# Keys and queries of six head pairs, transposed into one PSUM bank, copied by ScalarE and placed by two transfers

## The chip, the cores and the metric

The kernel runs on one core of a Trainium2 chip. Times are device microseconds of one execution, and the metric is their median over several runs: 278.72 us before the change, of three runs of 278.40, 278.72 and 280.70. One more execution was profiled. A core has TensorE (PE; its weight loads are shown as PEld), VectorE (DVE), ScalarE (ACT), GpSimd (POOL) and SyncE (SP). Matmuls write to PSUM, a memory of banks of 2 KB for each of 128 partitions; the other engines copy from there to SBUF. POOL, SP and ACT also issue DMA transfers.

## What is computed

Attention in which each query sees only some chunks of keys, and behind it a feed-forward layer. Shapes: 4 batches, 8 heads, 768 tokens, head dimension 64; the layer has 512 inputs and 2048 hidden units.

```python
k_chunks = k.reshape(B, H, nc, chunk, D)          # 24 chunks of 32 keys
k_min, k_max = np.min(k_chunks, axis=3), np.max(k_chunks, axis=3)
ub = np.sum(np.maximum(q[:, :, :, None, :] * k_min[:, :, None], 
                       q[:, :, :, None, :] * k_max[:, :, None]), axis=-1)
ub = np.where(causal, ub, -1e9)
top_chunks = np.argsort(ub, axis=-1)[..., -6:]
scores = scale * q @ k.T                          # where chunk selected and causal
out = softmax(scores) @ v
h = np.maximum(x @ w_in, 0.0)                     # x: out of all heads, 3072 x 512
return h * h @ w_out
```

## The kernel before

The work is cut into 32 pairs of heads: a batch, a half of its tokens (384), and two heads, in the order of `slots` (L208). Four pairs make a half batch (a group). The kernel's order is written out by hand: `tile_...` records for each engine its instructions in the order in which the Python calls stand, and each engine runs its own list in that order, waiting where an operand isn't there. Pairs are counted from 0; "slot s" is the turn of the main loop (L681) for pair s.

In slot s stand, by calls in this order: scores and exponentials of pair s (`step_E`, L395: matmuls into `ps`, ScalarE's `Exp` to `e`, for some parts a causal mask on POOL), the bounds of pair s+1 (`step_U`, L345), the output product of pair s-1 (`step_F`, L420: `po`, then a reciprocal and a product on VectorE to `x`), more scores, the selection of pair s+1 (`step_V`, L368: transposes `qt`, copied by VectorE beside the queries at L393 and L394), and the transposes of pair s+2 (`step_P`, L336). Between them `f1` puts pieces of the feed-forward layer from a queue: four matmuls of an up-projection (`ph`, L522; then `Relu` on ScalarE, square on VectorE at L528), or four of a down-projection (`py`, L538).

What becomes of a pair's keys and queries, for pairs 4 to 11: `step_T` (L235) transposes them on TensorE, 16 small matmuls, into two tiles, `tk` and `tq`, of one PSUM bank each; tokens stand there in the order (j p), four interleaved runs, and not (p j) as they are wanted. From PSUM four things are made. `relus_T` (L262): ScalarE writes relu(-q) and relu(q), in token order, to `qr` (L271). `extrema` (L212): VectorE reduces each chunk of 32 keys to its minimum and maximum (L216, L217) and multiplies them with a mask into `kbd` (L218). `place` (L273, the copies are at L276): VectorE copies the keys, and ScalarE the queries, head by head in token order to `kqs`, from which the score matmuls read; head 0 lies in partitions 64 to 127, head 1 in 0 to 63, while in PSUM head 0 is in 0 to 63. The bounds are matmuls of `qr` with `kbd` (L354); VectorE takes the eight largest of them (L361) and compares (L362, `nsel`).

Where the parts stand: `step_P` does `step_T` and, from pair 6 on, `step_T2` (L255), which is relus, extrema, both placings. For pair 9 the transposes are in slot 7 and the rest is written out in slot 8 (L713 to L728), between transposes of `x` (`x_T`, L460) and their copies (L472). Pairs 0 to 5 have code of their own. Pairs from 12 on are transposed by DMA from SP (`tr`, L302) into `kqT`, placed by two transfers for four pairs (`place_dma`, L286), and their relus are VectorE's, from SBUF (`relus`, L293, L299 and L300); the transfers of pairs 12 to 15 are issued in slots 9 to 11.

PSUM has eight banks: pool `psS` three (tag "ps"), `psF` two, `psY` one ("py"), `psA` two ("att"; also for `ub`, `qt`, `po`). `step_P` puts keys and queries of pairs 6 to 8 into psY and psS, those of pairs 9 to 11 into psS and psA.

Of the kernel before, what the change touches and what calls it, by code (L numbers as in the profile page):

```python
# [9 lines left out]
BF16 = mybir.dt.bfloat16  # L10
AX = mybir.AxisListType
ALU = mybir.AluOpType
# [5 lines left out]
HB = HT * 128  # L18
# [10 lines left out]
ORDER = ((0, 0), (1, 0), (0, 1), (1, 1), (2, 0), (2, 1), (3, 0), (3, 1))  # L29
# [3 lines left out]
TP = 4  # L33
# [6 lines left out]
def kernel(  # L40
# [9 lines left out]
    nc = tc.nc  # L50
    B, H, S, D = q.shape
    NC = S // CH
    NT = S // 128
    NP = H // 2
# [7 lines left out]
    work = ctx.enter_context(tc.tile_pool(name="work", bufs=2))  # L62
# [32 lines left out]
    def packed(n, g):  # L95
        return nat_of(n, g)[0:PP, :].rearrange("p (h x) -> p h x", h=H)
# [73 lines left out]
    for g in range(4):  # L170
        for j in range(HT):
            c = 13 + g + 4 * j
# [35 lines left out]
    slots = [(b, half, p) for b, half in ORDER for p in range(NP)]  # L208
    NS = len(slots)
    st = {}  # L210

    def extrema(kt, s):  # L212
        b, half, p = slots[s]
        km = work.tile([128, 2, 12], BF16, tag="km", name="km")
        kv = kt.rearrange("r (j c e) -> r c j e", j=TP, c=12)
        nc.vector.tensor_reduce(km[:, 0, :], kv, axis=AX.XY, op=ALU.min)  # L216
        nc.vector.tensor_reduce(km[:, 1, :], kv, axis=AX.XY, op=ALU.max)  # L217
        nc.vector.tensor_mul(  # L218
            kbds[b % 2][:, p, :, :, 12 * half:12 * half + 12], hmask,
            km.unsqueeze(2).to_broadcast([128, 2, 2, 12]))  # L220

    def in_order(x):

        return x.rearrange("r (j p) -> r p j", j=TP)

    def by_token(x):
        return x.rearrange("r (p j) -> r p j", j=TP)
# [7 lines left out]
    def step_T(s, kp, qp):  # L235

        b, half, p = slots[s]
        t = st.setdefault(s, {})
        for n, (pool, tag) in zip("kq", (kp, qp)):
            x = t[n] = pool.tile([128, HB], BF16, tag=tag, name="t" + n)  # L240
            if n == "q" and s < NP:
                for j in range(HT):
                    nc.tensor.matmul(
                        x[:, 128 * j:128 * (j + 1)],
                        lhsT=qn0[:, j, p, 1:3, :].rearrange("p h d -> p (h d)"),
                        rhs=ident, is_transpose=True, start=True, stop=True)
                continue
            for hh in range(2):
                for j in range(TP):
                    nc.tensor.matmul(  # L250
                        x[D * hh:D * hh + D, PP * j:PP * j + PP],
                        lhsT=packed(n, s // NP)[:, 2 * p + hh, D * j:D * j + D],
                        rhs=ident[0:PP, 0:PP], is_transpose=True, start=True, stop=True)

    def step_T2(s):  # L255
        relus_T(s)
        extrema(st[s]["k"], s)
        if s >= NP:
            place(s, "k", nc.vector.tensor_copy)
            place(s, "q", nc.scalar.copy)  # L260

    def relus_T(s):  # L262
        b, half, p = slots[s]
        t = st[s]
        qr = t["qr"] = work.tile([128, 2, HB], BF16, tag="qr", bufs=3, name="qr")
        c = 128 * (1 - half)
        for w in range(2):
            o, i = qr[:, w, c:], t["q"][:, c:]
            if s >= NP:
                o, i = by_token(o), in_order(t["q"])[:, c // TP:, :]  # L270
            nc.scalar.activation(o, i, ACT.Relu, scale=(-1.0, 1.0)[w])  # L271

    def place(s, n, copy, h0=0, h1=2):  # L273
        b, half, p = slots[s]
        for h in range(h0, h1):
            copy(by_token(kqs[b % 2][QROW[h]:QROW[h] + D, h, p, 2 * half + "kq".index(n), :]),  # L276
                 in_order(st[s][n][D * h:D * h + D]))

    tT = {}
# [11 lines left out]
                in_=half_T(g)[D * h:D * h + D])  # L291

    def relus(s):  # L293
        g, p = s // NP, s % NP
        qT = tT[g][:, p, 1, :]
        c = 128 * (1 - ORDER[g][1])
        t = st.setdefault(s, {})
        qr = t["qr"] = work.tile([128, 2, HB], BF16, tag="qr", bufs=3, name="qr")
        nc.vector.tensor_scalar(qr[:, 0, c:], qT[:, c:], -1.0, 0.0, op0=ALU.mult, op1=ALU.max)  # L299
        nc.vector.tensor_scalar_max(qr[:, 1, c:], qT[:, c:], 0.0)  # L300
# [31 lines left out]
    F, Y, A = (psF, "ph"), (psY, "py"), (psA, "att")  # L332

    S_ = (psS, "ps")

    def step_P(s):  # L336
        if s // NP >= ON_PE:
            relus(s)
            return
        step_T(s, *((S_, Y) if s == NP + 1 else (F, Y) if s < NP + 2 else  # L340
                    (Y, S_) if s < 2 * NP + 1 else (S_, A)))
        if s >= NP + 2 and s != 2 * NP + 1:
            step_T2(s)

    def step_U(s):  # L345
        b, half, p = slots[s]
# [113 lines left out]
    def x_T(hb, g, pt, us=(0, 1)):  # L460

        if (hb, g) not in pts:
            pts[hb, g] = pt[0].tile([128, 2, HB], BF16, tag=pt[1], name="pt")
        for u in us:
            for j in range(HT):
                nc.tensor.matmul(
                    pts[hb, g][:, u, 128 * j:128 * (j + 1)],
                    lhsT=xs[hb][:, j, 128 * (2 * g + u):128 * (2 * g + u + 1)],
                    rhs=ident, is_transpose=True, start=True, stop=True)
# [80 lines left out]
    def fill(n, act):  # L550
        for _ in range(n):
            if queue:
                queue.pop(0)(act)
# [127 lines left out]
    for s, (b, half, p) in enumerate(slots):  # L681
        if s < NP:
            continue
        hb = s // NP
        nb = len(BANKS[half])
        hf = nb // 2
        quota = [((4, 4, 4, 4) if hb == 1 else (8, 6, 7, 7))[p]]
        for fn, *a in first.get(s, ()):
            fn(*a)
        if ON_PE - 1 <= hb < 2 * B - 1 and p == (2 if hb < ON_PE else 1):  # L690
            parts.extend(step_K(hb + 1))

        def f1():
            if quota[0] and queue:
                quota[0] -= 1
                fill(1, True)

        if s == NP:
            for n in range(hf):
                step_E(s, 0, n)  # L700
            step_F(s - 1, 0)
            step_F(s - 1, 1)
            relus_T(s + 1)
            x_T(0, 1, F, (0,))
            x_copy(0, 1, 0, 1, nc.vector.tensor_copy)
            busy(8, *A)
            x_T(0, 1, F, (1,))
            x_copy(0, 1, 1, 2, nc.vector.tensor_copy)
            push(0)
            extrema(st[s + 1]["k"], s + 1)  # L710
            place(s + 1, "k", nc.vector.tensor_copy)
            place(s + 1, "q", nc.scalar.copy)
        if s == 2 * NP:  # L713
            for n in range(hf):
                step_E(s, 0, n)
            relus_T(s + 1)
            place(s + 1, "q", nc.scalar.copy)
            x_T(1, 0, A)
            x_copy(1, 0, 0, 2, nc.vector.tensor_copy)
            step_F(s - 1, 0)  # L720
            step_F(s - 1, 1)
            f1()
            f1()
            x_T(1, 1, A)
            x_copy(1, 1, 0, 2, nc.scalar.copy)
            push(1)
            extrema(st[s + 1]["k"], s + 1)
            place(s + 1, "k", nc.vector.tensor_copy)  # L728
        if p == 0 and hb > 2:
            step_F(s - 1, 0)  # L730
            step_F(s - 1, 1)
            step_X(hb - 1, False)
        else:
            f1()
        if s > NP and s != 2 * NP:
            for n in range(hf):
                step_E(s, 0, n)
        k1()
        f1()
        if p == 0 and hb > 2:  # L740
# [74 lines left out]
```

## Time and profile before

| | |
|---|---|
| runs | 278.40, 278.72, 280.70 us; median 278.72 |
| profiled execution | 278.57 us, of which the profile's span is 276.9 |
| granted TensorE clock | 1.0 throughout |
| instructions | 6716 |
| DMA | 32.05 MB, 116 GB/s in the mean |

A row of the timeline has a start and a length in us from the span's start, the engine, the line, the operation, output and inputs, the shape, how many instructions were merged into the row, and in brackets how long the engine had been idle and for whom it waited. Ends of matmuls are modelled, so rows of TensorE overlap a little. A row of the windows has the stretch, its length, then for each engine its busy time and number of instructions, the granted clock, the mean number of busy DMA engines as a share of 16 (over 1 where several packets are in flight in one engine), and GB/s. A row of DMA issues has output and input, the queue that issued it, how many, KB each, and the median time from issue to landing in us. The line of the chain gives the share of each item in the chain of waits that ended last in a stretch.

### The profile page before, as it was taken

How to read it: one execution, taken by the hardware profiler on the slowest of the kernel's cores; microseconds unless marked ns; L12 is line 12 of the kernel's file. 1: busy time of each engine (PE TensorE's matmuls, PEld its weight loads, DVE VectorE, ACT ScalarE, POOL GpSimd, SP SyncE). 2: the span in 40 equal slices, each digit the busy share in tenths (PEclk: the TensorE clock that was granted, in tenths of full speed). 3: DMA queues.
4: the chain of work that ended last, by engine and by line, in shares of the span. 5: the costliest groups of instructions: out<-in, count | busy, mean ns of one | idle time of the engine just before them, and what ended most of it. 6: DMA issues, size and time to landing. Idle time of an engine off the chain costs nothing.

```text
span 276.9 us, 6716 instructions
## 1 busy us (share of the span) xinstructions
PE 259.0 (94%) x2497; PEld 163.3 (59%) x2497; DVE 168.8 (61%) x645; ACT 181.9 (66%) x400; POOL 92.1 (33%) x137
## 2 busy tenths in 40 slices
PE   7687898899999999999999999999999999999994
PEld 6466555556666566655565566745565566655543
DVE  6687999656994368635894378616883455413411
ACT  6798889588975787835675777825674777615500
POOL 8796356316532016521551116701121111000000
PEclk9999999999999999999999999999999999999999
DMA  7999999959999249998599459996423200111002
GB/s 132 142 204 212 182 214 208 138 66 139 156 182 146 71 115 151 123 162 151 115 143 129 114 104 141 127 130 163 101 63 59 76 2 0 40 39 40 38 38 76
DMA packets 98272, 32.05 MB, mean 116 GB/s; under 512 B 84640, under 2 KB 93984, under 8 KB 98240
## 3 DMA queue, kind: packets, MB, share of 16 engines
q0 software_dynamic: 64720, 14.42, 61.7%
q1 hardware_dynamic: 32432, 16.88, 28.8%
q10 hardware_dynamic: 1088, 0.33, 0.5%
q8 instruction: 19, 0.31, 0.5%
q14 instruction: 13, 0.11, 0.1%
HBM read 27.26 MB, written 6.29 MB: 121 GB/s over the span
## 4 chain that ended last, share of the span: by engine, by line
PE 68%; DVE 13%; DMA 8%; ACT 5%; issue 2%; POOL 1%; SPq 1%; ACTq 0%; POOLq 0%
PE py L538 25%; PE ph L522 22%; PE ps L407 9%; PE po L432 7%; DMA qn<-in_q_dram 3%; DMA kn<-in_k_dram 3%; DVE h L528 2%; ACT e L412 2%; DVE kq L276 2%; DMA xT<-x 1%; DVE km L319 1%; ACT ht L526 1%; SPq L482 1%; DVE x L442 1%; ACT ob L544 1%
## 5 line engine op out<-in xcount | busy, mean ns | idle before, releaser
L412 ACT ACTIVATE e<-ps 128x512 bf16<-128x512 f32 x192 | 96.8, 550 | 26.6 <-PE ps L407 26.5
L522 PE MATMUL ph<-xT,w_in 128*128 128x384 bf16 x512 | 99.2, 326 | 0.6 <-DMA xT<-x 0.3
L538 PE MATMUL py<-w_out,h 128*128 128x512 bf16 x368 | 88.5, 379 | 1.2 <-ACT ob L544 0.9
L526 ACT ACTIVATE ht<-ph 128x384 bf16<-128x384 f32 x128 | 62.6, 499 | 27.3 <-PE ph L522 25.7
L416 POOL TENSOR_SCALAR_AFFINE_SELECT e<-e 128x384 bf16<-128x384 bf16 x64 | 34.5, 543 | 137.5 <-ACT e L412 137.5
L528 DVE TENSOR_TENSOR h<-ht 128x384 bf16<-128x384 bf16 x128 | 46.3, 374 | 43.5 <-ACT ht L526 43.3
L522 PEld LDWEIGHTS <-w_in 128*128 128x128 bf16 x512 | 47.4, 97 | 30.3 <-issue 1.4
L407 PE MATMUL ps<-kq 128*128 128x384 bf16 (+2 forms) x320 | 56.4, 278 | 2.8 <-ACT e L412 1.2
L538 PEld LDWEIGHTS <-h 128*128 128x128 bf16 x368 | 34.9, 97 | 35.3 <-issue 1.7
L407 PEld LDWEIGHTS <-kq 128*128 128x128 bf16 x320 | 26.3, 97 | 14.4 <-issue 2.6
L432 PEld LDWEIGHTS <-e 128*128 128x128 bf16 x672 | 25.6, 98 | 7.3 <-issue 2.0
L361 DVE MAX8 m<-ub 128x8 f32<-128x24 f32 (+1 forms) x160 | 16.7, 171 | 20.6 <-PE ub L354 19.7
L432 PE MATMUL po<-vn,e 128*128 128x65 bf16 x672 | 26.9, 194 | 1.4 <-POOL e L416 0.8
L544 ACT COPY ob<-py 128x512 f32<-128x512 f32 x19 | 11.1, 585 | 22.7 <-PE py L538 22.3
L442 DVE TENSOR_TENSOR x<-po,r 128x384 bf16<-128x384 f32 x32 | 17.8, 557 | 1.1
L393 DVE COPY kq<-qt 64x384 bf16<-64x384 bf16 (+1 forms) x28 | 8.8, 315 | 12.4 <-PE qt L389 12.4
L105 POOL DMA_DIRECT2D kn<-in_k_dram x15 | 13.3, 888 | 0.2
L105 POOL DMA_DIRECT2D qn<-in_q_dram x15 | 13.3, 886 | 0.0
L319 DVE TENSOR_TENSOR km<-km 128x384 bf16<-128x384 bf16 (+3 forms) x40 | 11.5, 287 | 1.1
L121 POOL DMA_DIRECT2D vn<-in_v_dram x12 | 10.7, 903 | 2.0 <-DVE kq L383 1.5
L354 PE MATMUL ub<-kbd,qr 128*128 128x48 bf16 (+1 forms) x160 | 9.6, 180 | 1.9 <-DVE kbd L218 1.0
L354 PEld LDWEIGHTS <-qr 128*128 128x128 bf16 x160 | 7.7, 96 | 4.2 <-ACT kq L276 1.3
(67 smaller groups left out, 198.8 us busy)
## 6 DMA issues: line engine op xcount, KB each, us to landing
out_dram<-ob SPq DMA_DIRECT2D x23, 256.0 KB, 2.2
kq<-kqT SPq DMA_DIRECT2D x10, 384.0 KB, 5.2
w_in<-in_moe_w_in_dram POOLq DMA_DIRECT2D x2, 1024.0 KB, 13.2
w_out<-in_moe_w_out_dram POOLq DMA_DIRECT2D x2, 1024.0 KB, 18.2
kn<-in_k_dram POOLq DMA_DIRECT2D x15, 128.0 KB, 6.0
qn<-in_q_dram POOLq DMA_DIRECT2D x15, 128.0 KB, 5.9
vn<-in_v_dram POOLq DMA_DIRECT2D x12, 128.0 KB, 9.2
vn<-in_v_dram POOLq DMA_DIRECT2D x4, 384.0 KB, 8.2
```

Source lines behind the costliest of these rows:

```text
L105: nc.gpsimd.dma_start(out=nat_of(n, g)[:, DM * j:DM * j + DM].rearrange("p (h d) -> p h d", d=D), in_=rows(n, *ORDER[g], 0, H)[:, 128 * j: ...
L354: nc.tensor.matmul(ub[:, j - j0], lhsT=st[s]["qr"][:, w, 128 * j:128 * (j + 1)], rhs=kbds[b % 2][:, p, w, :, 0:ncs], start=False, stop=(j ...
L361: nc.vector.max(out=m8[:, j, hh, :], in_=ub[:, j - j0, hh, :])
L407: nc.tensor.matmul(ps[:, at:at + 128 * m], lhsT=kqs[b % 2][:, hh, p, 2 * (j // HT), 128 * (j % HT):128 * (j % HT + 1)], rhs=qc(s, hh)[:, c ...
L412: nc.scalar.activation(e[:, 512 * n + lo:512 * n + hi], ps[:, lo:hi], ACT.Exp, scale=float(scale))
L416: nc.gpsimd.affine_select(out=d, in_=d, compare_op=ALU.is_ge, fill=0.0, base=0, channel_multiplier=-1, pattern=[[0, 3], [1, 128]])
L432: nc.tensor.matmul(po[:, hh, i, :], lhsT=t["e"][hh][:, c:c + 128], rhs=vn[b % 2][:, 2 * p + hh, j, :], start=(j == 0), stop=(j == iq))
L442: nc.vector.tensor_mul(x[:, :, 128 * p:128 * (p + 1)].rearrange("p j (h d) -> p h j d", h=2), po[:, :, :, 0:D], r.to_broadcast([128, 2, HT ...
L522: nc.tensor.matmul(ph[:, 0:HB], lhsT=w_in[:, ki, 128 * f:128 * (f + 1)], rhs=xT[:, ki, :], start=(ki == 0), stop=(ki == NKI - 1))
L526: nc.scalar.activation(ht, ph[:, 0:HB], ACT.Relu)
L528: nc.vector.tensor_mul(h, ht, ht)
L538: nc.tensor.matmul(py[t], lhsT=h2[hb, f][:, 128 * t:128 * (t + 1)], rhs=w_out[:, f, :], start=(f == 0), stop=(f == NFI - 1))
```

## The change

For pairs 6 to 11 (s >= NP + 2, with NP = 4):

- `step_T` transposes keys and queries into one tile `tkq` of [128, 2, 384], one PSUM bank; it lies in psY for pairs 6 to 8 and in psS for 9 to 11, and psA is no longer used for it.
- `stage` (new): ScalarE copies the tile at once, with the tokens brought to their order, to `kqp` in SBUF (two buffers), and SP issues two transfers, one a head, of [64, 2, 384] from there to `kqs`.
- `from_stage` (new): VectorE makes the two relus from the copy, and then the extrema, by a reduction over one axis, since tokens of a chunk are adjacent now.
- `relus_T` and both `place` of these pairs are gone. For pair 9, `stage` stands where its relus and queries' placing stood in slot 8, and `from_stage` where its extrema and keys' placing stood.

TensorE's list of instructions stays the same but for the tile that the transposes write and the waits; VectorE's has for each of these pairs two relus more and two copies fewer, ScalarE's one copy in place of two relus and two copies, SP's two transfers more.

```diff
+            if s < NP + 2:
+                x = pool.tile([128, HB], BF16, tag=tag, name="t" + n)
+            else:
+                if n == "k":
+                    both = t["kq"] = pool.tile([128, 2, HB], BF16, tag=tag, name="tkq")
+                x = both[:, "kq".index(n)]
...
+    def stage(s):
+        b, half, p = slots[s]
+        x = st[s]["stage"] = work.tile([128, 2, HB], BF16, tag="kqp", bufs=2, name="kqp")
+        nc.scalar.copy(x.rearrange("r n (p j) -> r n p j", j=TP),
+                       st[s]["kq"].rearrange("r n (j p) -> r n p j", j=TP))
+        for h in range(2):
+            nc.sync.dma_start(
+                out=kqs[b % 2][QROW[h]:QROW[h] + D, h, p, 2 * half:2 * half + 2, :],
+                in_=x[D * h:D * h + D])
+
+    def from_stage(s):
+        b, half, p = slots[s]
+        x = st[s]["stage"]
+        halves(s, x[:, 1])
+        extrema(x[:, 0], s, "r (c e) -> r c e", AX.X)
...
+    def halves(s, qT):
+        c = 128 * (1 - slots[s][1])
+        qr = t["qr"] = work.tile([128, 2, HB], BF16, tag="qr", bufs=3, name="qr")
         nc.vector.tensor_scalar(qr[:, 0, c:], qT[:, c:], -1.0, 0.0, op0=ALU.mult, op1=ALU.max)
         nc.vector.tensor_scalar_max(qr[:, 1, c:], qT[:, c:], 0.0)
...
         step_T(s, *((S_, Y) if s == NP + 1 else (F, Y) if s < NP + 2 else
-                    (Y, S_) if s < 2 * NP + 1 else (S_, A)))
+                    (Y, Y) if s < 2 * NP + 1 else (S_, S_)))
         if s >= NP + 2 and s != 2 * NP + 1:
-            step_T2(s)
+            stage(s)
+            from_stage(s)
...
         if s == 2 * NP:
...
-            relus_T(s + 1)
-            place(s + 1, "q", nc.scalar.copy)
+            stage(s + 1)
...
-            extrema(st[s + 1]["k"], s + 1)
-            place(s + 1, "k", nc.vector.tensor_copy)
+            from_stage(s + 1)
```

More of the change, by code (lines that the diff above doesn't have):

```diff
@@ L210, with extrema @@
     st = {}
-    def extrema(kt, s):
+    def extrema(kt, s, form="r (j c e) -> r c j e", axis=AX.XY):
         b, half, p = slots[s]
         km = work.tile([128, 2, 12], BF16, tag="km", name="km")
-        kv = kt.rearrange("r (j c e) -> r c j e", j=TP, c=12)
-        nc.vector.tensor_reduce(km[:, 0, :], kv, axis=AX.XY, op=ALU.min)
-        nc.vector.tensor_reduce(km[:, 1, :], kv, axis=AX.XY, op=ALU.max)
+        kv = kt.rearrange(form, c=12, **({"j": TP} if "j" in form else {}))
+        nc.vector.tensor_reduce(km[:, 0, :], kv, axis=axis, op=ALU.min)
+        nc.vector.tensor_reduce(km[:, 1, :], kv, axis=axis, op=ALU.max)
         nc.vector.tensor_mul(
@@ L239, in step_T @@
         for n, (pool, tag) in zip("kq", (kp, qp)):
-            x = t[n] = pool.tile([128, HB], BF16, tag=tag, name="t" + n)
+            if s < NP + 2:
[4 more added lines that the diff above has]
+                x = both[:, "kq".index(n)]
+            t[n] = x
             if n == "q" and s < NP:
@@ L293, in relus @@
     def relus(s):
-        g, p = s // NP, s % NP
-        qT = tT[g][:, p, 1, :]
-        c = 128 * (1 - ORDER[g][1])
+        halves(s, tT[s // NP][:, s % NP, 1, :])
+    def halves(s, qT):
+        c = 128 * (1 - slots[s][1])
         t = st.setdefault(s, {})
```

## The prediction

> **What bounds the kernel now.** I read the page first, then the chain of waits, the busy time of each engine by stage, the timelines of the engines, and the DMA issues by window.
>
> ```profile
> span 276.9 us, 6716 instructions
> PE 259.0 (94%) x2497; PEld 163.3 (59%) x2497; DVE 168.8 (61%) x645; ACT 181.9 (66%) x400; POOL 92.1 (33%) x137
> PE 68%; DVE 13%; DMA 8%; ACT 5%; issue 2%; POOL 1%; SPq 1%; ACTq 0%; POOLq 0%
> ```
>
> The span is TensorE's: 94% busy, 68% of the chain. What can be won is TensorE's idle time where the change acts, and what can be lost is any new wait of TensorE. The change touches pairs 6 to 11, counted from 0; pair s is transposed at the end of slot s-2 (pair 9: staged inside slot 8). So slots 4 to 9 matter, about 25 to 70 us. These are their windows (columns: window, length, then busy time of PE, PEld, DVE, ACT, POOL, then granted clock, DMA share, GB/s); the first three run from the end of one pair's transposes to the end of the next pair's, slots 5, 6 and 7:
>
> ```profile
> 31.92:37.25 5.33, 4.87 (x61) 3.16 (x58) 5.14 (x16) 4.77 (x12) 2.63 (x5) 1.00 1.53 194
> 37.25:42.63 5.38, 4.82 (x60) 3.08 (x58) 5.14 (x19) 4.93 (x13) 3.81 (x5) 1.00 1.22 225
> 42.63:48.85 6.22, 5.35 (x63) 3.28 (x60) 6.00 (x23) 5.25 (x13) 3.94 (x6) 1.00 1.39 200
> 48.85:54.00 5.15, 4.26 (x41) 2.66 (x42) 3.66 (x10) 3.49 (x7) 2.44 (x4) 1.00 3.14 138
> 54.00:66.00 12.00, 11.92 (x122) 7.32 (x121) 6.61 (x27) 8.97 (x21) 3.57 (x5) 1.00 0.78 97
> ```
>
> In slots 5 to 7 VectorE is the fullest (5.14 of 5.33, 5.14 of 5.38, 6.00 of 6.22), ScalarE not far behind, TensorE idle for 0.46, 0.56 and 0.87. In slot 8's first part TensorE idles 0.89, and from 54 us it is saturated. The DMA share is above 1 throughout the first four windows: transfers are always queued there. The chain inside 27 to 49.2 us says the same:
>
> ```profile
> by line: DVE kq L276 20.0%; DVE h L528 19.2%; DVE km L216 9.6%; DVE m L361 8.6%; DVE km L217 8.5%; DVE x L442 7.5%; DVE kbd L218 6.2%; DVE nsel L362 4.2%; DVE kq L394 4.0%; issue 3.9%; DVE kq L393 3.8%; DVE xT L472 1.6%; DVE r L441 1.6%; PE
> ```
>
> L276, the placing of the keys that the change removes, is its largest item. All the idle time from 31.92 to 54 is 2.78 us, so no rearrangement here is worth more than that.
>
> **The change, part by part.** First VectorE and ScalarE, from slots 6 and 7:
>
> ```profile
> 38.13 0.56 DVE L216 TENSOR_REDUCE km<-tk 128x12 bf16<-128x384 bf16 x1
> 38.61 0.55 DVE L217 TENSOR_REDUCE km<-tk 128x12 bf16<-128x384 bf16 x1
> 39.19 0.18 DVE L218 TENSOR_TENSOR kbd<-hmask,km 128x48 bf16<-128x48 bf16 x1
> 39.40 1.14 DVE L276 COPY kq<-tk 64x384 bf16<-64x384 bf16 x2
> 44.58 0.18 DVE L218 TENSOR_TENSOR kbd<-hmask,km 128x48 bf16<-128x48 bf16 x1
> 44.79 1.12 DVE L276 COPY kq<-tk 64x384 bf16<-64x384 bf16 x2
> 48.60 0.34 DVE L393 COPY kq<-qt 64x384 bf16<-64x384 bf16 x1
> 78.40 0.25 DVE L299 TENSOR_SCALAR qr<-kqT 128x384 bf16<-128x384 bf16 x1
> 78.57 0.25 DVE L300 TENSOR_SCALAR qr<-kqT 128x384 bf16<-128x384 bf16 x1
> 78.74 0.62 DVE L528 TENSOR_TENSOR h<-ht 128x384 bf16<-128x384 bf16 x2
> ```
> ```profile
> 37.35 0.66 ACT L271 ACTIVATE qr<-tq 128x256 bf16<-128x256 bf16 x2
> 38.04 0.96 ACT L276 COPY kq<-tq 64x384 bf16<-64x384 bf16 x2
> 53.30 0.80 ACT L472 COPY xT<-pt 128x768 bf16<-128x768 bf16 x1 [0.92 <-PE pt L466]
> 68.16 0.92 ACT L271 ACTIVATE qr<-tq 128x384 bf16<-128x384 bf16 x2
> ```
>
> VectorE loses the two copies (1.12) and gains two relus from SBUF; that form stands at L299 and L300, 0.34 from the first's start to the next instruction (78.40 to 78.74). The two reductions stay; none in the trace reads SBUF, so I keep their 1.06 (38.13 to 39.19). Net: 0.78 less VectorE work a pair. ScalarE loses two relus and two copies (0.66 + 0.96 = 1.62) and gains one copy of 128x768 from PSUM; the nearest row is L472, same size and direction, 0.80, though read without a stride (the strided L276 costs 0.48 for half the elements, so 0.96 bounds it above). Net: 0.7 to 0.8 less a pair.
>
> [...] No run here shows a reduction from SBUF yet.
>
> But the order is worth more than the amount. Before, the reductions started on the transposes in PSUM. Now ScalarE's copy stands between them, and the relus stand ahead of them on VectorE. TensorE's rows:
>
> ```profile
> 39.42 0.25 PE L354 MATMUL ub<-kbd,qr 128*128 128x24 bf16 x4 [0.35 <-DVE kbd L218]
> 41.82 0.28 PE L389 MATMUL qt<-ident,nsel 128*128 128x128 bf16 x2 [0.20 <-DVE nsel L362]
> 43.29 0.38 PE L407 MATMUL ps<-kq 128*128 128x384 bf16 x2
> 44.81 0.31 PE L354 MATMUL ub<-kbd,qr 128*128 128x48 bf16 x6 [0.32 <-DVE kbd L218]
> 49.09 0.60 PE L407 MATMUL ps<-kq 128*128 128x384 bf16 x4 [0.24 <-DVE kq L393]
> 50.67 0.53 PE L432 MATMUL po<-vn,e 128*128 128x65 bf16 x12 [0.65 <-DVE xT L472]
> 53.10 1.89 PE L538 MATMUL py<-w_out,h 128*128 128x512 bf16 x8
> 56.53 0.60 PE L407 MATMUL ps<-kq 128*128 128x384 bf16 x4
> ```
>
> Slot 6, by these rows: transposes end 37.25; ScalarE starts on them at 37.35; copy to 38.15; relus to 38.51 (0.02 between engines); reductions to 39.57; kbd 0.18, to 39.75; bound matmuls (L354) 0.05 later at 39.80, where they stood at 39.42. So TensorE waits 0.38 longer there. Behind it on TensorE stand an up-projection, the output product, another up, a score matmul, and qt (L389); the 0.20 that qt waited for nsel goes, since VectorE is now 0.40 ahead behind kbd. The slot ends between 42.63 and 42.81. The cycle transposes, copy, relus, reductions, bounds, next transposes has replaced VectorE's load as the limit: slots 5 and 6 win nothing. I take +0.1 each.
>
> Slot 7: copy 42.73 to 43.53, relus to 43.89, reductions to 44.95, kbd to 45.13. Before, VectorE was free at 45.91; it is now 0.78 ahead, and reaches L393 at 47.82, not 48.60. TensorE's bounds are at 45.18, not 44.81, but its idle 0.87 was mostly elsewhere. The next scores (49.09) waited for L393, so they come 0.55 to 0.78 earlier: I take -0.7.
>
> Slot 8: the output product at 50.67 waited 0.65 for a copy of xT, since the pool "att" had its other bank held by the transposed queries of pair 9. In the changed program these are in "ps" instead, and the instruction's only VectorE wait is for L393's pair of copies. That frees 0.65. The changed bank of psY or psS adds no wait: ScalarE's one copy empties it.
>
> Now the transfers. Each pair adds two, 64 rows of 1536 bytes, 96 KB, issued from SP when the copy ends.
>
> ```profile
> kq<-oneh SPq DMA_DIRECT2D x2, 144.0 KB, 6.7
> w_out<-in_moe_w_out_dram POOLq DMA_DIRECT2D x1, 1024.0 KB, 17.1
> kq<-kqT SPq DMA_DIRECT2D x2, 384.0 KB, 6.1
> kq<-kqT SPq DMA_DIRECT2D x2, 384.0 KB, 4.6
> ```
>
> The rows come from windows at 2.7, 32, 76 and 101 us. No small transfer from SP runs while the loads of POOL's queue are backed up as at 32 us. The same placing, four times as large, took 4.6 with the engines free and 6.1 beside loads; a smaller one in a free stretch must be below 4.6. The upper end is 6.7, at the crowded start. I take 4.0 (3 to 6.7), nearer to the 4.6 scaled down and then raised by 6.1/4.6. The deadline: pair 7's copy ends at 38.15 and its scores are at 43.29, 5.1 later; pair 8, 43.53 to 48.31, 4.8. So it is hidden, by about 0.8, under one slot of TensorE's work. The second transfer serves only the second head, half a slot later.
>
> [...]
>
> What the placings cost others: three pairs of them (6, 7, 8) run ahead of the second half of w_out.
>
> ```profile
> 32.51 0.90 POOL L567 DMA_DIRECT2D w_out<-in_moe_w_out_dram  x1 [0.48 <-ACT qr L271]
> 66.16 4.56 SPq L303 DMA_TRANSPOSE kqT<-qn  x3
> 76.13 1.30 SPq L289 DMA_DIRECT2D kq<-kqT  x2
> 80.40 0.28 PE L354 MATMUL ub<-kbd,qr 128*128 128x48 bf16 x5 [0.55 <-DVE kbd L325]
> ```
>
> Its second half landed at 49.6 (32.51 + 17.1) and is first used at 53.10 by the down-projection, which would now come at 53.10 - 0.7 - 0.65 + 0.2 = 51.95. 192 KB at the 4.6 us for 768 KB is 1.15 us a pair, so three put it at 53.0 at the latest, 49.6 at the earliest; I take 52.1, a cost of 0.15 (0 to 1.1).
>
> SP's order: placings of 6 to 9, a store, placings of 10, a store, three key transposes, placings of 11, three query transposes, the big placing of pairs 12 to 15. The query transposes ran at 66.16; now they stand behind pair 11's copy (68.16 + 0.8) and two issues of 0.65, so at 70.3, some 4 later. Who waits: relus at 78.40 and the placing at 76.13. They landed just ahead of 76.13; if the queue is less crowded they land near 77, so I cost nothing, with 0 to 1 as bounds. Against it stands the 0.55 that TensorE waits at 80.40 for VectorE, which pair 11's lighter work may remove.
>
> Sum: 0.2 - 0.7 - 0.65 + 0.15 = -1.0. From 54 us TensorE is full (11.92 of 12.00), so this is carried to the end. The profiled execution took 278.57 (span 276.9 and 1.67 around it): 277.57, forecast 277.6. The median of the runs, 278.72, is 0.15 above the profiled one.
>
> **The rivals.** *The gain is eaten.* w_out lands at 53.0, or pairs 9 and 11, where the loads are dense, are placed a little late: 278.5 to 279.5, say 278.8. For it: a DMA share of 3.14 in 48.85 to 54. Against: the 0.8 of slack.
>
> *The placings are late.* If a placing lands more than 4.9 us after its copy, TensorE, which works in order, stops at that pair's scores with up-projections, bounds and the next transposes behind it. Pair 7 is covered by pair 6's delay; pairs 6, 8 and 9 each pay the excess (9's copy follows slot 8's first scores, its own scores stood at 56.53; I take the same 4.9). From 5.25 the kernel is slower than before; at the 6.7 of kq<-oneh it is 3 x 1.8 - 1.0 = +4.4, 283.0; at 5.9 +2.0, 280.6. Middle 282. For it: the queue is fullest exactly there. Against: the row at 76.13 carries four times the bytes in 6.1. The extreme, a placing queued behind all loads issued ahead (the 17.1 of w_out), would cost over 10 us.
>
> *All idle time goes.* If the copy were quicker or VectorE had more slack than I see, 2.78 from 31.92 to 54 and the 0.55 at 80.40: 278.57 - 3.3 = 275.3. Against: the 0.8 that the bounds wait in each slot by my own sum.
>
> That the change does nothing is no rival: the instructions differ as the diff says.
>
> **How the numbers follow.** Forecast 0.46, its own range 276.9 to 278.4; eaten 0.22; late placings 0.24, of which 0.02 is the extreme; all idle gone 0.08. About 1%, 2.8 us, is what a measurement here tells from no change. Faster by that: the last case and a tail, 0.10. Slower: late placings above 281.5 and a tail of the eaten case, 0.26. Same: 0.64. The range leaves out most of the fastest case and the worst of the late one: 276.0 to 283.0.
>
> **What would show it.** Right: L276 gone from VectorE's chain at 27 to 49; the wait of L354 for kbd grown to 0.7 or so; slots 5 and 6 as long as before; scores of pair 8 near 48.5; kq<-kqp landing in 3 to 5 us; no score matmul waiting for a DMA. Wrong: score matmuls that wait for kq<-kqp, a down-projection that waits for w_out, VectorE idle at 77 us for kqT, or slots 5 and 6 shorter than 5.2.

## The result, and the profile after

Twelve executions of the changed kernel had a median of 282.21 us, twelve of the kernel before 279.68 us; the ratio is 1.0114, interval 1.0087 to 1.0142. The change makes the kernel slower by 1.1%, where the prediction had 0.4% faster. The profiled execution took 281.93 us with a span of 280.2, against 278.57 and 276.9: 3.3 us more. From the page of the changed kernel, the span, the busy time of the engines and the chain by engine:

```profile
span 280.2 us, 6703 instructions
PE 258.3 (92%) x2472; PEld 164.6 (59%) x2497; DVE 165.0 (59%) x645; ACT 177.0 (63%) x382; POOL 91.9 (33%) x137
PE 73%; DMA 8%; DVE 7%; ACT 5%; issue 2%; SPq 2%; POOL 1%; ACTq 0%; POOLq 0%; DVEq 0%
```

VectorE has 3.8 us less to do and ScalarE 4.9, as intended. TensorE's busy time is nearly the same (258.3 against 259.0 us, with 25 of its matmuls missing from this trace), so the 3.3 us are idle time of TensorE or time at a lower clock. The place is read best from one event of each pair, the start of the `nsel` row on VectorE, when that pair's limits are ready. The table subtracts its time in the kernel before (30.84 us for pair 5, 47.15 for 8, 56.30 for 9, 74.04 for 11, 81.40 for 12, 91.38 for 13):

| lateness, us | pair 5 | 6 | 7 | 8 | 9 | 11 | 12 | 13 |
|---|---|---|---|---|---|---|---|---|
| changed kernel | +0.25 | +0.42 | +0.54 | +2.17 | +1.36 | +0.78 | +2.72 | +4.28 |

The change acts from pair 6 on, so pair 5's 0.25 is from run to run. Three steps stand out: +1.63 at pair 8 (slot 7), +1.94 at pair 12 (slot 11), +1.56 at pair 13 (slot 12). Between them slots 8 to 10 win 1.39. Here is TensorE's timeline at those steps (start, length, instruction, and in brackets the idle time before it and what ended that):

```profile
35.63 0.25 PE L379 MATMUL ub<-kbd,qr 128*128 128x24 bf16 x4 [1.64 <-DVE kbd L218]
39.45 0.39 PE L432 MATMUL ps<-kq 128*128 128x384 bf16 x2 [0.20 <-DMA kq<-kqp]
46.66 0.39 PE L432 MATMUL ps<-kq 128*128 128x384 bf16 x2 [1.90 <-DMA kq<-kqp]
51.26 0.60 PE L432 MATMUL ps<-kq 128*128 128x384 bf16 x4 [0.58 <-DVE kq L418]
...
81.75 0.20 PE L379 MATMUL ub<-kbd,qr 128*128 128x48 bf16 x1 [0.85 <-DVE qr L323]
83.13 0.28 PE L379 MATMUL ub<-kbd,qr 128*128 128x48 bf16 x5 [1.18 <-DVE kbd L349]
```

**Slot 7.** The scores of pair 7 waited 1.90 us for their placing. The DMA issues in a window at 39 to 41 us, where POOL's queue moved 0.42 MB, and in one at 60 to 63 us, where it moved 0.14 MB (last column: median us from issue to landing):

```profile
vn<-in_v_dram POOLq DMA_DIRECT2D x2, 128.0 KB, 14.1
kq<-kqp SPq DMA_DIRECT2D x2, 96.0 KB, 7.2
```
```profile
kq<-kqp SPq DMA_DIRECT2D x2, 96.0 KB, 2.4
```

The two transfers of a pair, 96 KB each, landed in 2.4 us in the later window (DMA share 0.86, 97 GB/s) and in 7.2 beside the loads of the earlier one (1.25, 211 GB/s). By the prediction's rows the scores need them about 5 us after ScalarE's copy.

**Slots 11 and 12.** On SP's queue the placing of pair 11 stands ahead of the query transposes of pairs 12 to 15, and it waits for ScalarE's copy (first fence, SP's queue). VectorE's first relu of pair 12 then waits for the transposes (second fence). The third fence has TensorE's windows on a grid of 3.41 us, the length of the half-clock stretch from 83.93 (columns: window, length, busy time of PE, PEld, DVE, ACT, POOL, granted clock, DMA share, GB/s):

```profile
70.40 2.20 SPq L275 DMA_DIRECT2D kq<-kqp  x2
72.69 4.57 SPq L327 DMA_TRANSPOSE kqT<-qn  x3
```
```profile
81.44 0.26 DVE L323 TENSOR_SCALAR qr<-kqT 128x384 bf16<-128x384 bf16 x1 [2.29 <-DMA kqT<-qn]
```
```profile
77.11:80.52 3.41, 3.41 (x24) 2.00 (x23) 1.92 (x6) 2.63 (x7) 0.92 (x2) 1.00 2.16 149
80.52:83.93 3.41, 1.38 (x14) 0.82 (x13) 2.32 (x15) 1.44 (x3) 1.86 (x3) 1.00 1.25 116
83.93:87.34 3.41, 3.41 (x39) 2.61 (x38) 1.58 (x6) 1.31 (x3) 0.00 (x0) 0.50 1.41 184
87.34:90.75 3.41, 3.41 (x50) 2.61 (x50) 2.24 (x9) 2.50 (x6) 1.35 (x2) 1.00 1.42 162
```

The transposes are issued at 72.69, where the kernel before had 66.16. TensorE, which takes its list in order, stopped at pair 12's bounds. It was busy for 1.38 of 3.41 us, and the window behind that ran at a granted clock of 0.50. At a clock of 0.50 a window of 3.41 us loses up to 1.7 us of work (an estimate from these two numbers), and the lateness grows by 1.56 at pair 13.

### The profile page after: what moved, and what is told of

The parts are those of the page before. It is cut to its first block, busy times and chain, and to the rows that moved or that the text cites. A ratio compares the mean times of both kernels' runs of the same rounds, so it can differ in the third digit from the quotient of the medians.

```text
span 280.2 us, 6703 instructions
## 1 busy us (share of the span) xinstructions
PE 258.3 (92%) x2472; PEld 164.6 (59%) x2497; DVE 165.0 (59%) x645; ACT 177.0 (63%) x382; POOL 91.9 (33%) x137
## 4 chain that ended last, share of the span: by engine, by line
PE 73%; DMA 8%; DVE 7%; ACT 5%; issue 2%; SPq 2%; POOL 1%; ACTq 0%; POOLq 0%; DVEq 0%
PE py L563 27%; PE ph L547 23%; PE ps L432 10%; PE po L457 7%; DMA qn<-in_q_dram 3%; DMA kq<-kqp 3%; DMA kqT<-qn 2%; PE idle L641 2%; ACT e L437 1%; ACT ht L551 1%; ACT ob L569 1%; DVE h L553 1%; PE ub L379 1%; SPq L327 1%; PE qt L414 1%
## 5 line engine op out<-in xcount | busy, mean ns | idle before, releaser
L563 PE MATMUL py<-w_out,h 128*128 128x512 bf16 x343 | 83.9, 379 | 2.6 <-ACT ob L569 0.9
L457 PEld LDWEIGHTS <-e 128*128 128x128 bf16 x672 | 26.3, 99 | 6.7 <-issue 1.4
L457 PE MATMUL po<-vn,e 128*128 128x65 bf16 x672 | 27.8, 196 | 0.9 <-POOL e L441 0.8
L343 DVE TENSOR_TENSOR km<-km 128x384 bf16<-128x384 bf16 (+3 forms) x40 | 10.8, 271 | 1.1
```

What stands on the lines that cost most here:

```text
L457: nc.tensor.matmul(po[:, hh, i, :], lhsT=t["e"][hh][:, c:c + 128], rhs=vn[b % 2][:, 2 * p + hh, j, :], start=(j == 0), stop=(j == iq))
L563: nc.tensor.matmul(py[t], lhsT=h2[hb, f][:, 128 * t:128 * (t + 1)], rhs=w_out[:, f, :], start=(f == 0), stop=(f == NFI - 1))
```

## The experiments

Two theories stood at the start. *Transfers*: the loss is in pair 7's landing, the order on SP's queue, and the half clock behind it. *Compute order*: the loss is ScalarE's copy and VectorE's relus standing ahead of the bounds in each staged slot. All ratios are against the kernel before on the same chip, with 95% intervals.

**e1: the order on SP's queue.** The transposes are put ahead of pair 11's placing:

```diff
-  first.setdefault(s0 + i // HT, []).append((tr, g, "kq"[i // HT], i % HT))
+  first.setdefault(s0, []).append((tr, g, "kq"[i // HT], i % HT))
```

> All six transposes of pairs 12 to 15 are issued before the placing of pair 11; nothing else differs from the changed kernel. Transfers theory (of the 3.3 us by which the changed kernel's profiled span is longer, about 2 are the relu of pair 12 that waited 2.29 us for kqT, and 1.6 the stretch at half the granted clock right behind it): the wait at the relu of pair 12 is below 0.5 us, no half clock near 84 us, pair 13's limits (nsel) no more than 1.5 us later than in the kernel before, ratio to before 1.000 to 1.004 (what pairs 6 and 7 lose stays). Compute-order theory (the loss is ScalarE's copy ahead of the bounds in every staged slot): nothing is moved there, so the ratio stays 1.009 to 1.013.

Measured: 279.92 us, ratio 1.0000 (0.9965 to 1.0034). Pair 12 is 0.19 earlier than before, without a wait at its relu and without a half clock (mean granted clock 1.000). This one line takes away the whole 1.1%, as far as the interval tells. It says nothing yet of pairs 6 to 8, which still lose 1.30 from pair 5 to pair 8; slots 8 to 11 win that back.

**e2, e3, e8: which pairs.** A set `STAGED` chooses between the new and the old way for each pair; e8 is e2 with e1's line.

```diff
+  STAGED = range(2 * NP + 1, 3 * NP)       # e2, e8: 9 to 11
+  STAGED = range(NP + 2, 2 * NP + 1)       # e3: 6 to 8
...
+  if s in STAGED:
       stage(s)
       from_stage(s)
+  else:
+      step_T2(s)
```

> Only pairs 9 to 11 are staged; 6 to 8 are transposed and placed as before the change. Transfers theory: nothing is lost in slots 5 to 7, and slot 8's gain (no wait for a bank) stays, but pair 11's placing still stands ahead of the query transposes, so the relu of pair 12 still waits 1.5 to 2.5 us and the ratio is 1.003 to 1.010, its height set by whether the clock halves. Compute-order theory: half of the staged slots, so 1.004 to 1.007 with no wait at the relu of pair 12 that matters.

> Only pairs 6 to 8 are staged; 9 to 11 as before the change. Transfers theory: pair 7's scores wait 1 to 2 us for its placing, part of which is won back in slots 8 to 11 where waits of VectorE and the banks take it up; the query transposes are issued as before, pair 12's relu waits for nothing, no half clock; ratio 1.000 to 1.004. Compute-order theory: half of the loss, 1.004 to 1.007.

> Pairs 9 to 11 staged, 6 to 8 as before the change, and the query transposes of pairs 12 to 15 issued ahead of pair 11's placing. Transfers theory: keeps what the run with pairs 9 to 11 alone showed up to pair 11 (limits 1.17 us earlier than before), and pair 12's relu waits for nothing, so span 275.5 to 276.2 where no half clock falls in, ratio 0.994 to 0.998: faster than both kernels. Compute-order theory: 1.002 to 1.006, as half of the staged slots remain.

Measured: e2 280.05 us, 1.0021 (0.9985 to 1.0056); e3 282.35 us, 1.0076 (1.0040 to 1.0113); e8 277.34 us, **0.9945 (0.9924 to 0.9967)**, faster than both kernels. In e2 pair 11 is 1.17 us early, then the relu of pair 12 waits 1.67 us for the transposes and the clock halves (0.67 in the mean of 80 to 84 us): pair 13 is 2.06 late, 3.2 lost in two slots. In e8, with the order right, pair 12 is 1.21 early and stays so. e2's ratio lies below the ranges of both theories, though its wait is the one that the transfers theory named. e3's lies above both (1.0076, against 1.004 and 1.007 at most), with an interval that holds compute order's. Its scores waited for placings of pairs 7 and 8 (1.43 and 0.89), and behind the second wait a half clock followed at about 54 us (0.71 in the mean of 52 to 56), which neither theory had.

So the pairs differ in sign: 9 to 11 gain about 0.5% (e8), 6 to 8 lose 0.5 to 0.8% (e1 against e8; e3 alone), and the order on SP's queue costs 0.6 to 1.1% (e6 below; e2 against e8; the changed kernel against e1).

**e6: the order alone, in the kernel before.** Nothing of the change but two transfers behind pair 11's relus, into a tile that nobody reads:

```diff
+  def extra(s):
+      x = st[s]["qr"]
+      for h in range(2):
+          nc.sync.dma_start(out=dump[s % 2][D * h:D * h + D], in_=x[D * h:D * h + D])
...
+  if s == 3 * NP - 1:
+      extra(s)
```

> The kernel before the change, with two transfers of 64 rows of 1536 bytes from pair 11's relus into a tile nobody reads, issued from SP at the place of the changed kernel's placing of pair 11; the compute is that of before. Order theory: the issue waits for ScalarE's relus of pair 11 and the three query transposes wait behind it on SP, so they are issued 2 to 5 us later than before, the relu of pair 12 waits 1 to 2.5 us for kqT, in some executions the clock halves behind it, ratio 1.004 to 1.013. Compute-order theory: no change, 0.998 to 1.002.

> The same kernel as the run with extra transfers behind pair 11, for its trace. Order theory: query transposes of pairs 12 to 15 issued 2 to 5 us later than before, relu of pair 12 waits 1 to 2.5 us for kqT.

Measured: 280.47 us, 1.0055 (1.0032 to 1.0079). The rows are from a second profiled execution, as the first took 925 us. SP's queue, VectorE and TensorE in it:

```profile
69.61 1.61 SPq L350 DMA_DIRECT2D dump<-qr  x2
71.34 4.77 SPq L303 DMA_TRANSPOSE kqT<-qn  x3
```
```profile
80.29 0.26 DVE L299 TENSOR_SCALAR qr<-kqT 128x384 bf16<-128x384 bf16 x1 [1.28 <-DMA kqT<-qn]
```
```profile
82.34 0.28 PE L361 MATMUL ub<-kbd,qr 128*128 128x48 bf16 x5 [1.54 <-DVE kbd L325]
```

Lateness goes from +0.52 at pair 11 to +1.94 at pair 12 and +3.52 at pair 13, with a half clock from about 83 us (0.65 in the mean of 84 to 88): the two steps of the changed kernel (+1.94, +1.56) as +1.42 and +1.58, in a kernel whose compute is that of before.

**e5: TensorE kept busy.** The changed kernel with 32 matmuls that nobody reads ahead of pair 12's bounds.

```diff
+  if s == 3 * NP - 1:
+      busy(32)
   step_U(s + 1)
```

> The changed kernel, and ahead of pair 12's bounds 32 more matmuls of 128x128 on TensorE whose result nobody reads. If the half clock behind 84 us comes from TensorE's idle time while it waits for the late query transposes: the relu of pair 12 still waits 2 us or more for kqT, but no half clock follows, pair 13's limits stand 2 to 3 us late against before instead of 4.3, and the ratio falls from 1.011 to 1.005 to 1.008. If the half clock comes for another reason it stays near 84 us, and the ratio stays at 1.011 or rises to 1.016 by the matmuls.

Measured: 281.82 us, 1.0106 (1.0063 to 1.0149). The relu waited 1.67 us and no half clock followed there: pair 12 stands at +3.93 and pair 13 too, where the changed kernel lost 1.56 between them. The ratio did not fall to the 1.005 to 1.008 expected of that cause. The one trace shows two reasons: the matmuls take 1.95 us themselves, and in this execution the clock halved at another place, behind the wait of pair 7's scores (the same grid of windows):

```profile
43.34:46.75 3.41, 1.34 (x22) 0.76 (x22) 2.76 (x10) 2.00 (x5) 2.01 (x3) 1.00 1.27 193
46.75:50.16 3.41, 3.41 (x18) 1.93 (x19) 1.16 (x8) 1.36 (x3) 0.87 (x3) 0.50 1.28 224
```

**e7: traffic alone.** The kernel before, with two transfers of the same size for each of pairs 6 to 8, which nobody waits for.

The edit, shortened:

```diff
+  nc.sync.dma_start(
+      out=dump[s % 2][D * h:D * h + D],
+      in_=kqs[b % 2][QROW[h]:QROW[h] + D, h, p, 2 * half:2 * half + 2, :])
```

> The kernel before the change, with two transfers of 64 rows of 1536 bytes for each of pairs 6 to 8, read from the placed keys and queries into a tile nobody reads. Waiting theory: landings of 5.5 to 7.5 us, as those of the changed kernel, and ratio 0.998 to 1.002. Traffic theory (the added bytes delay the second half of w_out): the first down-projection waits 0.5 to 2 us for w_out, ratio 1.002 to 1.008.

Measured: 278.81 us, 0.9975 (0.9945 to 1.0005). They landed in 7.1 us (the DMA issues of 33 to 50 us), and the first down-projection waited for nothing:

```profile
w_out<-in_moe_w_out_dram POOLq DMA_DIRECT2D x1, 1024.0 KB, 20.7
dump<-kq SPq DMA_DIRECT2D x6, 96.0 KB, 7.1
```

`w_out` did land later, 20.7 us after its issue at 33.29 against 17.1 in the kernel before, just as its second half was first used (by the matmuls at 54.00). So the bytes cost no time here, but not by much.

**e4, e10: other hands for the placing.** Two VectorE copies from SBUF for all staged pairs (e4), two GpSimd copies for pairs 6 to 8 with the transposes first (e10). The edits, shortened:

```diff
-  nc.sync.dma_start(out=kqs[...], in_=x[D * h:D * h + D])
+  nc.vector.tensor_copy(kqs[...], x[D * h:D * h + D])     # e4, behind the reductions
+  nc.gpsimd.tensor_copy(kqs[...], x[D * h:D * h + D])     # e10
```

> ScalarE's one copy, the relus and the reductions from its copy in SBUF stay for pairs 6 to 11; the two transfers of each pair are replaced by two VectorE copies of 64x768 from SBUF. Transfers theory: no landing to wait for and SP's order as before, so all of the loss goes: ratio 0.995 to 1.001, with no wait of a score matmul above 0.5 us that was not there before. Compute-order theory: the bounds still wait for ScalarE's copy in each slot and VectorE has more to do, so the ratio stays above 1.008.

> All pairs staged, the query transposes first, and pairs 6 to 8 placed by two GpSimd copies of 64x768 from SBUF instead of two transfers. Landing theory: if a copy takes up to 2.4 us, both are done 4.8 us after ScalarE's copy, no later than the scores need them, and the ratio is 0.990 to 0.996; if one takes longer the scores wait as they do for the transfers and the ratio is 0.998 to 1.004. Compute-order theory: 0.997 to 1.003 whatever the copies take.

Measured: e4 279.80 us, 1.0001 (0.9974 to 1.0028); e10 279.78 us, 1.0000 (0.9971 to 1.0029). In neither does a score matmul wait for a placing, yet from pair 5 to pair 8 they lose 1.98 and 1.95 us, more than e1's 1.30. GpSimd's two copies took 1.70 us together, well inside the deadline:

```profile
40.22 1.70 POOL L279 COPY kq<-kqp 64x768 bf16<-64x768 bf16 x2 [0.23 <-ACT kqp L272]
```

For pairs 6 to 8 the transfers theory missed: with the landing gone their loss should have gone. But neither run is a clean test of it. e4's ratio is in that theory's range, as e4 also mends SP's order, and its copies are new work for VectorE. In e10 one relu stood still beside GpSimd's copy in slots 6 and 7, 0.86 and 0.88 us where e9 below has 0.22 and 0.25 (slot 6):

```profile
40.26 0.86 DVE L326 TENSOR_SCALAR qr<-kqp 128x256 bf16<-128x256 bf16 x1
```

**e9, e11, e12: landing and relus, two by two.** e9 is e1 without the placing of pairs 6 to 8; e11 is e1 with the relus of pairs 6 to 8 back on ScalarE, from its own copy; e12 has both. The edits, shortened (without the memset at the start of e9 and e12):

```diff
   # e9, e12
-  nc.sync.dma_start(...)
+  if s > 2 * NP:
+      nc.sync.dma_start(...)
   # e11, e12
-  halves(s, x[:, 1])
+  if s > 2 * NP:
+      halves(s, x[:, 1])
+  else:
+      for w in range(2):
+          nc.scalar.activation(qr[:, w, c:], x[:, 1, c:], ACT.Relu, scale=(-1.0, 1.0)[w])
```

> The kernel with all pairs staged and the query transposes first, but the placing of pairs 6 to 8 is left out: their keys and queries in kq stay zero, from a memset at the start. Copy, relus and reductions of these pairs stay in the changed order, so this is the change with placings that nobody waits for. Landing theory (pairs 6 to 8 cost by the landing of the placings): the wait of pair 7's scores is gone, slots 7 and 8 gain what the prediction said (about 1), pair 8's limits are no later than before, ratio 0.990 to 0.995, at or below that of the kernel with pairs 6 to 8 as before (0.9945). Compute-order theory (ScalarE's copy ahead of the bounds): pairs 6 to 8 still lose 0.5 us or more against that kernel, ratio 0.997 to 1.003.

> All pairs staged, the query transposes first, the placings by transfers; of pairs 6 to 8 the relus go back to ScalarE, which reads its own copy in SBUF, so that VectorE's reductions start right behind the copy, beside the relus. If pairs 6 to 8 lose by the relus on VectorE (in the run without placings the first of pair 6 took 0.96 beside GpSimd's 0.90 for the descriptors of w_out, and the bounds waited 1.74 for kbd): the bounds of pair 6 wait less than 0.8 us for kbd. If the landing of pair 7's placing is a second limit of its own, its scores still wait 1.5 us or more, pairs 6 to 8 together still lose 0.6 to 1.3 us, and the ratio stays at 0.997 to 1.002. If the landing only hides behind the late bounds, the ratio falls to 0.993 to 0.996.

> The same relus on ScalarE in the kernel that leaves out the placing of pairs 6 to 8 (their keys and queries in kq stay zero from a memset at the start, which makes the start some 4 us longer, so that what counts is the lateness from pair 5 on, and the ratio against that kernel's 1.0075). Relu theory: from pair 5 to pair 8 the limits fall back by no more than 0.5 us (1.28 with the relus on VectorE), and by pair 12 they have gained 0.8 to 1.5 (0.39 lost there is 0.11 gained with VectorE's relus), ratio 1.001 to 1.005. If it is the copy itself ahead of the reductions that costs: still 1 us or more from pair 5 to 8, ratio 1.006 to 1.010.

Measured: e9 281.60 us, 1.0075 (1.0049 to 1.0101); e11 279.01 us, 1.0002 (0.9969 to 1.0034); e12 280.60 us, 1.0040 (1.0013 to 1.0067). In e9 and e12 pair 5 is already 4.01 and 4.67 us late, from the memset at the start and, in e9, from a granted clock of 0.50 at 13.7 to 20.5 us. So their ratios can't be set beside the others; what counts is the change from pair 5 on:

| from pair 5, us | to pair 8 | to pair 12 |
|---|---|---|
| e1: VectorE relus, transfers | +1.30 | -0.09 |
| e9: VectorE relus, no placing | +1.28 | -0.11 |
| e11: ScalarE relus, transfers | +0.81 | +0.48 |
| e12: ScalarE relus, no placing | **-0.49** | **-1.98** |
| e8: pairs 6 to 8 as before the change | +0.07 | -1.42 |

In e2, e6 and e7, which also leave pairs 6 to 8 as before the change, the first number is -0.06, -0.23 and -0.16. So differences of some 0.3 us between two traces are scatter.

TensorE's waits in slots 5 to 7 of e9, e11 and e12, one fence each:

```profile
39.49 0.25 PE L387 MATMUL ub<-kbd,qr 128*128 128x24 bf16 x4 [1.74 <-DVE kbd L225]
44.99 0.25 PE L387 MATMUL ub<-kbd,qr 128*128 128x24 bf16 x4 [0.89 <-DVE kbd L225]
50.69 0.31 PE L387 MATMUL ub<-kbd,qr 128*128 128x48 bf16 x6 [1.04 <-DVE kbd L225]
```
```profile
39.93 0.39 PE L438 MATMUL ps<-kq 128*128 128x384 bf16 x2 [1.43 <-DMA kq<-kqp]
46.05 0.39 PE L438 MATMUL ps<-kq 128*128 128x384 bf16 x2 [1.48 <-DMA kq<-kqp]
51.80 0.60 PE L438 MATMUL ps<-kq 128*128 128x384 bf16 x4 [1.73 <-DMA kq<-kqp]
```
```profile
38.86 0.25 PE L393 MATMUL ub<-kbd,qr 128*128 128x24 bf16 x4 [0.45 <-DVE kbd L225]
44.10 0.25 PE L393 MATMUL ub<-kbd,qr 128*128 128x24 bf16 x4 [0.62 <-DVE kbd L225]
49.33 0.31 PE L393 MATMUL ub<-kbd,qr 128*128 128x48 bf16 x6 [0.58 <-DVE kbd L225]
```

Take the landing away and TensorE waits for the bounds instead; move the relus and the bounds come in time, and the scores of all three pairs wait 1.4 to 1.7 us for their landings. Against e12, by pair 8, the late bounds alone cost 1.77 us (e9), the landings alone 1.30 (e11), and both together 1.79 (e1). They lie beside each other, so removing one returns little, and each theory alone had to miss. Of the 1.77, 0.74 falls in slot 5, where VectorE's relu also stood still beside GpSimd (last section). No run separates that stall from the relus' place in the order.

**e13: both limits gone in a complete kernel.** e11, with VectorE placing pairs 6 to 8 from SBUF behind its reductions.

```diff
+  if s <= 2 * NP:
+      place_x(s, nc.vector.tensor_copy)
```

> A complete kernel with neither of the two limits of pairs 6 to 8: ScalarE copies and does their relus from its copy, VectorE reduces and places from it (two copies of 64x768 from SBUF behind kbd, 0.36 to 0.50 each in the run where VectorE places); pairs 9 to 11 are placed by transfers and the query transposes go first. Two-limits theory (a late bound and a late landing stood side by side, each enough to cost about 1): no score matmul waits for a placing, bounds wait less than 0.7 us for kbd, from pair 5 to pair 8 the limits lose no more than 0.3 us, by pair 12 they have gained 1 to 2, ratio 0.990 to 0.995. If something else in the staging of pairs 6 to 8 costs: 0.8 us or more lost from pair 5 to 8, ratio 0.997 to 1.002.

Measured: 278.74 us, 0.9974 (0.9953 to 0.9995). No score waits for a placing, and the bounds wait 0.36 to 0.61, as the two-limits theory expected. Its sizes missed: pair 8 has lost 1.15 since pair 5 (0.3 at most was expected), and pair 12 has gained only 0.33 (1 to 2). The wait has moved to the next VectorE result, the transposes of the limits (0.20 to 0.30 in the kernel before):

```profile
37.31 0.29 PE L427 MATMUL qt<-ident,nsel 128*128 128x128 bf16 x2 [0.27 <-DVE nsel L400]
43.04 0.28 PE L427 MATMUL qt<-ident,nsel 128*128 128x128 bf16 x2 [0.54 <-DVE nsel L400]
49.20 0.34 PE L427 MATMUL qt<-ident,nsel 128*128 128x128 bf16 x3 [0.92 <-DVE nsel L400]
```

Beside ScalarE's relus, placing these pairs costs 1.65 us by pair 12 when VectorE does it (e13's -0.33 against e12's -1.98) and 2.46 by transfers (e11's +0.48). As e12 starts later, these are sizes, not exact prices. e8, which leaves pairs 6 to 8 alone, is the best version found.

## Why the prediction was wrong

- **VectorE's and ScalarE's work: nearly right.** ScalarE's copy takes 0.80 us as taken from L472, the reductions 0.53 to 0.55 each from SBUF, as from PSUM. For VectorE six pairs at 0.78 would be 4.7 us less, and 3.8 was measured; relus of pairs 6 and 9 that took longer than 0.25 can account for the difference. The 1.06 us kept for the two reductions held: from the first reduction to `kbd` it is 1.04 in slot 6.
- **Slot 8: right.** Forecast -0.65 for the output product's bank; the lateness falls by 0.81 there, in the changed kernel and in e8.
- **w_out and the added bytes: the delay right, the missing wait in part luck.** Forecast +0.15 (0 to 1.1). `w_out` landed at 52.5 (issued at 32.85, 19.7 later), close to the 52.1 taken. Nobody waited, because the slots before ran late and its second half was first used at 54.47, not at 51.95.
- **Landing: the term mis-sized.** "I take 4.0 (3 to 6.7)" was 5.8 to 7.4 for pairs 6 to 8. The rival of late placings had the mechanism, but not its shape: pairs 6 and 8 hardly waited for their placings in the changed kernel, and pair 7, which it called covered by pair 6's delay, waited 1.90. That its 282 is near the 282.21 measured is chance: it let three pairs pay for their landings, while 1.94 + 1.56 us of the lateness at pair 13 came behind SP's order and 1.63 in slot 7. The row at 76.13 that spoke against it was of a time when POOL's loads themselves landed in 4 to 7 us, not in 11 to 20 as around 33 to 45 us; the nearest row by load was `kq<-oneh`, at 6.7. The rival's extreme, over 10 us behind all loads issued ahead, did not come: 7.2 beside loads that took 14.1.
- **Slots 5 to 7 as a whole: the sum failed in its order.** Forecast 0.1 + 0.1 - 0.7 = -0.5; the changed kernel shows +0.17, +0.12, +1.63. The extra 0.38 at the bounds was well sized (in e9, pair 7's transposes end at 42.35 and its bounds start at 44.99, 2.64 later, against 2.17 before), but it was taken as absorbed, and VectorE's earlier L393 was booked as a gain behind it. The -0.7 does not follow from the prediction's own rows: slot 7 had 0.87 of idle time, and a wait at the bounds that grows from 0.32 to 0.69 leaves 0.18 to win. With no landing at all (e9) these slots still lose 1.28. Only with neither limit (e12) does -0.49 come out, and then with ScalarE's relus, so that its nearness to -0.5 bears nothing out.
- **The order on SP's queue: the step that decided.** "so I cost nothing, with 0 to 1 as bounds". The prediction saw that the query transposes move by some 4 us and named who waits for them. They had landed just ahead of 76.13, so 4 later is about 80, behind the relus at 78.40; the prediction put "near 77" in its place, on the hope of a less crowded queue. They were issued 6.5 us later, as pair 11's transposes ended 1.36 late and the placing's two issues took 2.20 and not 1.3. They landed at 79 to 81 us, and the relu waited 2.29. e1 and e6 show this from both sides: ratio 1.0000 when the order alone is mended, 1.0055 when the order alone is spoilt.
- **The half clock: not in the prediction at all.** Its row at full clock for every window of the kernel before was read as a property of the kernel. Behind the half clock the lateness grew by 1.56 us in the profiled execution.

One gain was in no term of the forecast: the limits of pair 11 come 0.49 us earlier in slot 10 in all versions that place that pair by transfers. The traces point to ScalarE. In the kernel before it reached the `Relu` of the up-projection behind two relus and two copies of pair 11, in e8 behind one copy (the first row is before, the second e8):

```profile
70.08 0.87 ACT L526 ACTIVATE ht<-ph 128x384 bf16<-128x384 f32 x2
```
```profile
68.32 0.94 ACT L556 ACTIVATE ht<-ph 128x384 bf16<-128x384 f32 x2
```

TensorE's next up-projection stands 1.30 us behind its scores in e8 (68.50 to 69.80), where it was 1.59 (69.03 to 70.62). That is 0.29 of the 0.49. No run tests it, and the rest stays open.

## What to carry to other kernels

An issue that waits for compute held up what stood behind it in SP's queue (the query transposes were issued at 72.69 us, where they had been at 66.16): price the instructions behind such an issue by their new issue time plus a landing from a row with the same load on the engines (96 KB landed in 7.2 us beside the loads and in 2.4 later), not from the nearest row of the same kind. When a step's result has two uses (here the bounds and the scores), find the slack of both before booking a gain, since removing the wait you see can uncover the one beside it (with no landing, e9, pairs 6 to 8 still lost 1.28 us, where e1 lost 1.30). And judge a staging where it stands: with SP's order mended, the same edit won 0.5% at pairs 9 to 11, where TensorE had queued work (busy for 11.92 of 12.00 us from 54 us on in the kernel before), and lost as much at pairs 6 to 8.

## What the runs showed of the hardware

**The clock halved behind poorly used windows.** In the changed kernel's trace the half clock lasts 3.413 us, and the stretches of full clock on either side of it are 23 and 57 times as long; hence the grid of 3.41 us. The window ahead of the half clock had TensorE busy for 1.38 of 3.41 us, and in e5 it was 1.34. Two windows of 1.78 us in the changed kernel (from 32.73 and 42.97) and one of 1.81 in the kernel before (from 7.83) were followed by full clock. It also went either way on like figures: from 8 to 12 us TensorE was busy for 2.25 of 4.00 us in the kernel before, in the changed kernel and in e7, and only in e7 did a half clock follow (0.61 in the mean of 12 to 16). So these traces place no limit. (The clock's record begins 4.42 us into the span in the kernel before and 5.42 in the changed kernel.) The grid starts at another place in each of these traces, 1.01 us into the span in the kernel before, 2.01 in the changed kernel and 2.38 in e5, so one wait of 2 us may fall into one window or be split over two. By an estimate from their mean clocks (0.994 in the profiled execution with its one stretch, 0.982 at the lowest), eleven of twelve executions of the changed kernel had one to three, against 19 of 35 of the kernel before. They are a part of its spread from 280.56 to 284.72 us, not all of it: seven executions with one stretch each took 280.99 to 284.11.

**A VectorE relu from SBUF stood still beside some of GpSimd's work.** In the changed kernel, VectorE and GpSimd at 33 us:

```profile
33.11 1.26 DVE L323 TENSOR_SCALAR qr<-kqp 128x256 bf16<-128x256 bf16 x1 [0.76 <-ACT kqp L272]
```
```profile
32.85 0.90 POOL L592 DMA_DIRECT2D w_out<-in_moe_w_out_dram  x1 [0.47 <-DMA vn<-in_v_dram]
33.75 0.54 POOL L441 TENSOR_SCALAR_AFFINE_SELECT e<-e 128x384 bf16<-128x384 bf16 x1
```

The relu takes 0.23 us in the next slot. Here it ended at 34.37, 0.62 us behind the row that issues `w_out`, but only 0.08 behind GpSimd's next instruction, a causal mask. In e9 and e10 a relu at that place ended 0.09 behind the same mask (36.87 to 37.83 and 33.46 to 33.93 us); in e10 it had started after the end of the row that issues `w_out` (33.30). So the relu's end went with the mask's. Beside rows that issue a load it stood still in some cases and not in others: in the changed kernel the relu at 53.73 took 0.64 and ended 0.06 behind such a row, while the one at 45.40 took 0.25 in the middle of one. Reductions from SBUF beside the same work kept their 0.53 to 0.55 in the changed kernel, e9 and e10. In the changed kernel pair 6's limits were only 0.17 us later in that slot; in e12, with the relus on ScalarE, they were 0.47 earlier.
